# A cross network on one core: row halves that swap roles, one product split into seven smaller ones, and one-bank PSUM tiles

## The chip, the cores and the metric

The kernel runs on one core of a Trainium2 chip. Time is device time in microseconds (us) of one execution. The core has TensorE (matrix products, PE in the profile, its weight loads as PEld), VectorE (DVE), ScalarE (ACT), GpSimd (POOL) and SyncE (SP), each with its own queue of instructions worked off in order. All transfers of this kernel are issued from SyncE's queue.

## The reference

The input x0 has 16384 rows of 1024 elements in bf16. Six layers follow, each with a 1024x1024 weight matrix and a bias:

```python
x = x0
for l in range(6):
    proj = jnp.einsum('bd,de->be', x, ws[l]) + bs[l]
    x = x0 * proj + x
return x
```

So every layer is one product of 16384x1024 by 1024x1024, then an element-wise multiplication by x0 and an addition.

## The kernel before

The rows are worked in 16 pairs of two halves of 512 rows (`NPAIR`, `NB`). The data of a pair lie transposed in SBUF: 128 partitions of features, 8 blocks of features, 512 rows along the free dimension (`x0T`, and `xst` for the running x). A pair goes through all six layers before the next pair starts; a pair and layer together are called a step here, 96 of them.

In a step the 2x2 block product (two halves of the features by two halves of the rows, times two halves of the outputs) is done with seven half-size products instead of eight, in the manner of Strassen and Winograd. Each of the seven is 4 x 4 matmuls of 128x128 weights by 512 columns. With B(d, r) for feature half d and row half r, product 1 takes B(0,0), product 2 B(1,0), product 3 B(1,1), and products 5, 6, 7 and 4 take the differences T1 to T4, which VectorE makes (`emit_T`, lines 93 to 99): T1 = B(0,1) - B(0,0), T2 = B(1,1) - T1, T3 = B(1,1) - B(0,1), T4 = B(1,0) - T2. The weights of products 1, 2 and 4 are blocks of `ws`; those of 5, 6, 3 and 7 are combinations that VectorE makes once, in pair 0 (`emit_combo`, lines 126 to 132), for the layer that comes next, and saves to DRAM (`Lc`, line 106). All later pairs load seven weight tiles of 512 KB in each step through a ring of 12 buffers (`wring`, `prefetch_upto`, line 79), requested nine places ahead in the order of use.

The order in a step is 1, 5, 3, 2, 6, 7, 4. Matmuls are all on line 196. Product 1 starts two PSUM tiles of two banks each (`pA`); products 6, 7 and 4 add onto them one after the other, and after each of them ScalarE copies the running sum out (`evac`: line 205 without bias in pieces of 1024 columns, line 208 with bias in pieces of 512). Product 5 starts two other tiles (`pX`), product 3 adds onto them, and product 2 has the same pool's tiles after that. VectorE adds the evacuated parts (lines 235, 241, 250), multiplies by x0 (`final`, line 214) and adds the old x (line 223, in the last step line 219). In what follows "multiply" and "add" of a quarter (eh, n) are these two operations.

The queue of each engine is laid out in program order by the framework's scheduler, which may move instructions; semaphores are set by it. SyncE's queue holds the weight loads, the saves of combinations, per pair two transposing loads of x0 (lines 145 and 268), the output transpose (line 288) with two stores (line 291), and for the last pair four transposes (line 168) with four stores (line 280). A weight load waits until the product that used its ring slot has ended.

Of the kernel before, what the change touches and what calls it, by code (L numbers as in the profile page):

```python
# [16 lines left out]
def kernel(  # L17
# [19 lines left out]

    const = ctx.enter_context(tc.tile_pool(name="const", bufs=1))
# [7 lines left out]
    psA = ctx.enter_context(tc.tile_pool(name="psA", bufs=2, space=bass.MemoryType.PSUM))  # L46
    psX = ctx.enter_context(tc.tile_pool(name="psX", bufs=2, space=bass.MemoryType.PSUM))
    stage_ctx = ExitStack()
    w12_pool = stage_ctx.enter_context(tc.tile_pool(name="w12", bufs=2))
    xo_ctx = ExitStack()  # L50
    xo_pool = None

    Lc = dram.tile([L, 4, P, KH * H], BF16, name="Lc")
    CIDX = {5: 0, 6: 1, 7: 2, 3: 3}
# [11 lines left out]
    ORDER = [1, 5, 3, 2, 6, 7, 4]  # L66
    all_keys = [(pr, l, pid) for pr in range(NPAIR) for l in range(L) for pid in ORDER]
    key_pos = {k_: i for i, k_ in enumerate(all_keys)}
    is_dma = lambda k_: not (k_[0] == 0 and k_[2] in CIDX)
    PREF = 9  # L70
# [12 lines left out]
    def blk(t, dh, n):  # L83
        return t[:, n, dh * KH:(dh + 1) * KH, :]

    def emit_T(xsrc, which):
        B11, B12, B21, B22 = blk(xsrc, 0, 0), blk(xsrc, 0, 1), blk(xsrc, 1, 0), blk(xsrc, 1, 1)
        Ts = which["T"]
        for i in which["do"]:
            t_ = t_pool.tile([P, KH, NB], BF16, name=f"T{i}")  # L90
            Ts[i] = t_
            if i == 1:
                nc.vector.tensor_tensor(out=t_[:], in0=B12, in1=B11, op=SUB)  # L93
            elif i == 2:
                nc.vector.tensor_tensor(out=t_[:], in0=B22, in1=Ts[1][:], op=SUB)
            elif i == 3:
                nc.vector.tensor_tensor(out=t_[:], in0=B22, in1=B12, op=SUB)
            else:
                nc.vector.tensor_tensor(out=t_[:], in0=B21, in1=Ts[2][:], op=SUB)
# [4 lines left out]
    def flush_saves():  # L104
        for (l_, pid_, t_) in pending_saves:
            si = nc.sync.dma_start(Lc[l_, CIDX[pid_]].rearrange("p (k e) -> p k e", k=KH), t_[:])
            if state.get("last_dma") is not None:
                tc.add_manual_dep(si.ins, state["last_dma"].ins.name,
                                  mybir.DependencyInfo(mybir.DependencyClass.NoSync, mybir.DependencyReason.DATA),
                                  reason="combo save behind the urgent weight loads")  # L110
        pending_saves.clear()
# [8 lines left out]
    def emit_combo(l, pid):  # L120
        prefetch_upto(key_pos[(0, l, 4)] + 1)
        W11, W21, W22 = wtiles[(0, l, 1)], wtiles[(0, l, 2)], wtiles[(0, l, 4)]
        w12 = load_w12(l)
        t_ = wring.tile([P, KH, H], BF16, name="wp")
        if pid == 5:
            nc.vector.tensor_tensor(out=t_[:], in0=w12[:], in1=W22[:], op=ADD)  # L126
        elif pid == 6:
            nc.vector.tensor_tensor(out=t_[:], in0=wtiles[(0, l, 5)][:], in1=W11[:], op=SUB)  # L128
        elif pid == 3:
            nc.vector.tensor_tensor(out=t_[:], in0=W21[:], in1=wtiles[(0, l, 6)][:], op=SUB)  # L130
        else:
            nc.vector.tensor_tensor(out=t_[:], in0=W11[:], in1=w12[:], op=SUB)
        wtiles[(0, l, pid)] = t_
        pending_saves.append((l, pid, t_))

    wt0 = wring.tile([P, KH, H], BF16, name="wp")
    nc.sync.dma_start(wt0[:], w_src(0, 1))
    wtiles[(0, 0, 1)] = wt0
    load_w12(0)
    wt4 = wring.tile([P, KH, H], BF16, name="wp")  # L140
    nc.sync.dma_start(wt4[:], w_src(0, 4))
    wtiles[(0, 0, 4)] = wt4
    x0T_next = x0t_pool.tile([P, 2, KD, NB], BF16, name="x0T")
    for n in range(2):
        nc.sync.dma_start_transpose(out=x0T_next[:, n], in_=x0[n * NB:(n + 1) * NB, :])  # L145
    LK = L * KD
# [4 lines left out]
    for pid in (5, 6, 3, 7):  # L151
        emit_combo(0, pid)
    nc.gpsimd.tensor_copy(b_all[:], b_bf[:])
    Tn = {"T": {}, "do": (1, 2, 3, 4)}
    emit_T(x0T_next, Tn)
    prefetch_upto(PREF)
    flush_saves()

    for pr in range(NPAIR):
# [3 lines left out]
        xo_last = {"t": None, "regions": [], "xfin": None}  # L163

        def out_region(eh, n):
            if xo_last["t"] is None:
                xo_last["t"] = xo_pool.tile([P, 2, 2, KH, KH, P], BF16, name="xoS")
            ti = nc.sync.dma_start_transpose(out=xo_last["t"][:, eh, n].rearrange("p j k r -> p (j k) r"),
                                             in_=xo_last["xfin"][:, eh, n].rearrange("r j k p -> r (j k p)"))
            xo_last["regions"].append((eh, n))  # L170
            xo_last["tins"] = xo_last.get("tins", []) + [ti]
        for l in range(L):
            xsrc = x0T if l == 0 else xst
            Ts = Tn["T"]
            Tn = {"T": {}, "do": ()}
            rhs_of = {1: blk(xsrc, 0, 0), 2: blk(xsrc, 1, 0), 3: blk(xsrc, 1, 1), 4: Ts[4][:], 5: Ts[1][:], 6: Ts[2][:], 7: Ts[3][:]}
            bias_col = lambda eh, m: b_all[:, l * KD + eh * KH + m: l * KD + eh * KH + m + 1]
            if pr == 0 and l + 1 < L:
                prefetch_upto(key_pos[(0, l + 1, 4)] + 1)
                load_w12(l + 1)  # L180
            flush_saves()
            pA = [psA.tile([P, 2, NB], FP32, name="pa") for _ in range(2)]
            C1 = cb_pool.tile([P, KH, 2, NB], BF16, name="cb")
            C2 = cb_pool.tile([P, KH, 2, NB], BF16, name="cb")
            nxt_src = xst if l + 1 < L else None
            combos_next = pr == 0 and l + 1 < L

            def product(pid, pts, start):
                key = (pr, l, pid)
                prefetch_upto(key_pos[key] + PREF)  # L190
                wt = wtiles.pop(key) if not (pr == 0 and pid in (1, 2, 4)) else wtiles[key]
                rhs = rhs_of[pid]
                for m in range(KH):
                    for k in range(KH):
                        kw = {} if start else dict(skip_group_check=True)
                        nc.tensor.matmul(pts[m // 2][:, m % 2, :], lhsT=wt[:, k, m * P:(m + 1) * P], rhs=rhs[:, k, :],  # L196
                                         start=(start and k == 0), stop=(k == KH - 1), **kw)

            def evac(pts, bias_eh=None, dst=None):
                if dst is None:  # L200
                    e = ev_pool.tile([P, KH, NB], BF16, name="ev")
                    dst = e[:]
                if bias_eh is None:
                    for h in range(2):
                        nc.scalar.copy(out=dst[:, 2 * h:2 * h + 2, :], in_=pts[h][:])  # L205
                else:
                    for m in range(KH):
                        nc.scalar.activation(out=dst[:, m, :], in_=pts[m // 2][:, m % 2, :], func=IDENT,  # L208
                                             bias=bias_col(bias_eh, m), scale=1.0)
                return dst  # L210

            def final(Cb, eh, n):
                c = Cb[:, :, n, :]
                nc.vector.tensor_tensor(out=c, in0=c, in1=blk(x0T, eh, n), op=MULT)  # L214
                if last_pair and l == L - 1:
                    if xo_last["xfin"] is None:
                        xo_last["xfin"] = xst_pool.tile([P, 2, 2, KH, KH, P], BF16, name="xst")
                    v4 = lambda a: a.rearrange("r k (j p) -> r k j p", p=P)
                    nc.vector.tensor_tensor(out=xo_last["xfin"][:, eh, n].rearrange("r j k p -> r k j p"),  # L219
                                            in0=v4(c), in1=v4(blk(xsrc, eh, n)), op=ADD)  # L220
                    out_region(eh, n)
                else:
                    nc.vector.tensor_tensor(out=blk(xst, eh, n), in0=c, in1=blk(xsrc, eh, n), op=ADD)  # L223

            product(1, pA, True)
            P1s = evac(pA)
            pX = [psX.tile([P, 2, NB], FP32, name="px") for _ in range(2)]
            product(5, pX, True)
            P5s = evac(pX)
            product(3, pX, False)  # L230
            S53 = evac(pX, bias_eh=0)
            pX2 = [psX.tile([P, 2, NB], FP32, name="px") for _ in range(2)]
            product(2, pX2, True)
            P2s = evac(pX2, bias_eh=0)
            nc.vector.tensor_tensor(out=C1[:, :, 0, :], in0=P1s, in1=P2s, op=ADD)  # L235
            final(C1, 0, 0)
            if combos_next:
                emit_combo(l + 1, 5)
            product(6, pA, False)
            U2s = evac(pA)  # L240
            nc.vector.tensor_tensor(out=C1[:, :, 1, :], in0=U2s, in1=S53, op=ADD)  # L241
            final(C1, 0, 1)
            if nxt_src is not None:
                Tn["do"] = (1,)
                emit_T(nxt_src, Tn)
            if combos_next:
                emit_combo(l + 1, 6)
            product(7, pA, False)
            U3s = evac(pA, bias_eh=1)
            nc.vector.tensor_tensor(out=C2[:, :, 1, :], in0=U3s, in1=P5s, op=ADD)  # L250
            final(C2, 1, 1)
            if combos_next:
                emit_combo(l + 1, 3)
            product(4, pA, False)
            evac(pA, bias_eh=1, dst=C2[:, :, 0, :])
            final(C2, 1, 0)
            if nxt_src is not None:
                Tn["do"] = (2, 3, 4)
                emit_T(nxt_src, Tn)
# [63 lines left out]
```

## Time and profile before

| what | value |
|---|---|
| time, median of 3 runs | 2353.55 us (2353.24 to 2353.8) |
| span of the profiled execution | 2352.8 us, 0.75 us below the median |
| TensorE busy | 2312.4 us, 98% of the span |
| weight loads busy | 1052.7 us, 10752 loads, 98 ns each |
| VectorE busy | 1708.6 us, 73% |
| ScalarE busy | 1556.7 us, 66% |
| granted TensorE clock, mean | 0.997 of full speed |
| DMA | 457.96 MB, 67.0% of 16 engines' time |

A line of the costliest groups reads: line of the kernel, engine, operation, output tile <- input tiles, shapes, number of instructions, busy time in us, mean duration in ns, then the engine's idle time just before these instructions and what ended most of it. A line of waits reads: waiting engine, line, what it waited for, us in total, how often, the longest. In the timeline a row has start, duration, engine, line, operation, and in brackets the idle time before it. Matmuls overlap: a single record lasts 379 ns, while the next one starts long before its end, so the distance between starts tells the pace.

### The profile page before, as it was taken

To read this page: it belongs to the slowest core of one execution; us is meant where nothing else is said; L and a number is where in the kernel's file an instruction comes from. 1 tells how busy PE (TensorE), PEld (TensorE's weight loads), DVE (VectorE), ACT (ScalarE), POOL (GpSimd) and SP (SyncE) were. 2 spreads that over 40 slices of the span, in tenths; PEclk is the share of its full clock that TensorE was granted. 3 is DMA by queue.
4 is the path that set the end of the run, shared out by engine and by line. 5 is a ranking of instruction groups with operands and counts; after the bars stand their busy time and mean duration, and the time that the engine had idled before them with its cause. 6 is when DMAs were issued, how large, how long until landed. Compare 5 with 4: busy or idle time off the path is not lost.

```text
span 2352.8 us, 27562 instructions
## 1 busy us (share of the span) xinstructions
PE 2312.4 (98%) x10537; PEld 1052.7 (45%) x10752; DVE 1708.6 (73%) x1464; ACT 1556.7 (66%) x2113; POOL 1.2 (0%) x5
## 2 busy tenths in 40 slices
PE   7999999999999999999999999999999999999997
PEld 3444444444444444444444444444444444444443
DVE  5977767676777767676776767677776767777675
ACT  4666666666666666666666666666666666666665
POOL 0000000000000000000000000000000000000000
PEclk9999999999999999999999999999999999999998
DMA  7769485584956849568494774947749476594843
GB/s 226 203 210 256 152 216 196 161 253 154 228 184 171 241 154 240 171 177 235 153 259 153 178 233 152 259 152 190 221 152 260 153 198 214 155 257 152 226 153 86
DMA packets 599987, 457.96 MB, mean 195 GB/s; under 512 B 398128, under 2 KB 550704, under 8 KB 599856
## 3 DMA queue, kind: packets, MB, share of 16 engines
q1 hardware_dynamic: 599856, 456.20, 67.0%
q8 instruction: 85, 1.39, 0.2%
q14 instruction: 46, 0.38, 0.1%
HBM read 342.88 MB, written 46.14 MB: 165 GB/s over the span
## 4 chain that ended last, share of the span: by engine, by line
PE 96%; DVE 1%; DMA 1%; issue 1%; SPq 1%; ACT 0%; another core or an unknown queue 0%; DVEq 0%
PE pa L196 54%; PE px L196 42%; SPq L145 1%; DMA w_313<-in_ws_dram 0%; DMA wp<-in_ws_dram 0%; DVE cb L214 0%; DVE xst L219 0%; DVE xst L223 0%; ACT ev L208 0%; DVE cb L241 0%; DVE cb L250 0%; DVE cb L235 0%; DVE wp L128 0%; DVE T_247 L93 0%; DVE T_811 L93 0%
## 5 line engine op out<-in xcount | busy, mean ns | idle before, releaser
L196 PEld LDWEIGHTS <-wp 128*128 128x128 bf16 x10752 | 1052.7, 98 | 1283.8 <-issue 12.7
L208 ACT ACTIVATE ev<-px,b_all 128x512 bf16<-128x512 f32 x768 | 486.3, 684 | 201.3 <-PE px L196 193.3
L196 PE MATMUL px<-xst,wp 128*128 128x512 bf16 x2510 | 562.5, 379 | 2.7
L235 DVE TENSOR_TENSOR cb<-ev 128x2048 bf16<-128x2048 bf16 x96 | 117.6, 1225 | 594.2 <-ACT ev L208 594.2
L205 ACT CAST ev<-pa 128x1024 bf16<-128x1024 f32 x384 | 388.6, 1012 | 240.2 <-PE pa L196 230.8
L214 DVE TENSOR_TENSOR cb<-cb,x0T 128x2048 bf16<-128x2048 bf16 x384 | 467.8, 1221 | 6.3
L223 DVE TENSOR_TENSOR xst<-cb,xst 128x2048 bf16<-128x2048 bf16 x316 | 385.0, 1222 | 14.5
L208 ACT ACTIVATE ev<-pa,b_all 128x512 bf16<-128x512 f32 x384 | 243.1, 684 | 112.9 <-PE pa L196 108.2
L208 ACT ACTIVATE cb<-pa,b_all 128x512 bf16<-128x512 f32 x384 | 243.1, 684 | 88.4 <-ACT ev L208 48.4
L196 PE MATMUL pa<-xst,wp 128*128 128x512 bf16 x1254 | 287.3, 379 | 1.3
L205 ACT CAST ev<-px 128x1024 bf16<-128x1024 f32 x192 | 194.3, 1012 | 138.1 <-PE px L196 133.1
L241 DVE TENSOR_TENSOR cb<-ev 128x2048 bf16<-128x2048 bf16 x96 | 117.0, 1219 | 0.0
L250 DVE TENSOR_TENSOR cb<-ev 128x2048 bf16<-128x2048 bf16 x96 | 117.0, 1218 | 0.0
L196 PE MATMUL px<-x0T,wp 128*128 128x512 bf16 x501 | 112.4, 379 | 0.5
L223 DVE TENSOR_TENSOR xst<-cb,x0T 128x2048 bf16<-128x2048 bf16 x64 | 78.3, 1223 | 1.5
L196 PE MATMUL pa<-x0T,wp 128*128 128x512 bf16 x251 | 60.2, 391 | 12.9 <-DMA x0T<-in_x_dram 12.6
L130 DVE TENSOR_TENSOR wp<-wp 128x2048 bf16<-128x2048 bf16 x6 | 7.3, 1219 | 2.1 <-DMA wp<-in_ws_dram 2.1
L128 DVE TENSOR_TENSOR wp<-wp 128x2048 bf16<-128x2048 bf16 x6 | 7.3, 1219 | 0.0
L126 DVE TENSOR_TENSOR wp<-w_90,wp 128x2048 bf16<-128x2048 bf16 x1 | 1.2, 1226 | 8.2 <-DMA wp<-in_ws_dram 8.2
L93 DVE TENSOR_TENSOR T_111<-x0T 128x2048 bf16<-128x2048 bf16 x1 | 1.2, 1226 | 5.7 <-DMA x0T<-in_x_dram 5.7
L219 DVE TENSOR_TENSOR xst<-cb,xst 128x2048 bf16<-128x2048 bf16 x4 | 4.9, 1225 | 0.1
L196 PE MATMUL px<-T_247,wp 128*128 128x512 bf16 x16 | 3.6, 378 | 0.3 <-DVE T_247 L93 0.3
(783 smaller groups left out, 1858.9 us busy)
## 6 DMA issues: line engine op xcount, KB each, us to landing
wp<-Lc SPq DMA_DIRECT2D x360, 512.0 KB, 3.4
wp<-in_ws_dram SPq DMA_DIRECT2D x288, 512.0 KB, 3.7
out_dram<-x0T SPq DMA_DIRECT2D x30, 1024.0 KB, 9.8
Lc<-wp SPq DMA_DIRECT2D x24, 512.0 KB, 3.1
out_dram<-xoS SPq DMA_DIRECT2D x4, 512.0 KB, 4.7
w_90<-in_ws_dram SPq DMA_DIRECT2D x1, 512.0 KB, 4.7
x0T<-in_x_dram SPq DMA_TRANSPOSE x32, 7.3
w_130<-in_ws_dram SPq DMA_DIRECT2D x1, 512.0 KB, 5.0
```

The source lines that it names most:

```text
L128: nc.vector.tensor_tensor(out=t_[:], in0=wtiles[(0, l, 5)][:], in1=W11[:], op=SUB)
L130: nc.vector.tensor_tensor(out=t_[:], in0=W21[:], in1=wtiles[(0, l, 6)][:], op=SUB)
L145: nc.sync.dma_start_transpose(out=x0T_next[:, n], in_=x0[n * NB:(n + 1) * NB, :])
L196: nc.tensor.matmul(pts[m // 2][:, m % 2, :], lhsT=wt[:, k, m * P:(m + 1) * P], rhs=rhs[:, k, :], start=(start and k == 0), stop=(k == KH - ...
L205: nc.scalar.copy(out=dst[:, 2 * h:2 * h + 2, :], in_=pts[h][:])
L208: nc.scalar.activation(out=dst[:, m, :], in_=pts[m // 2][:, m % 2, :], func=IDENT, bias=bias_col(bias_eh, m), scale=1.0)
L214: nc.vector.tensor_tensor(out=c, in0=c, in1=blk(x0T, eh, n), op=MULT)
L219: nc.vector.tensor_tensor(out=xo_last["xfin"][:, eh, n].rearrange("r j k p -> r k j p"), in0=v4(c), in1=v4(blk(xsrc, eh, n)), op=ADD)
L223: nc.vector.tensor_tensor(out=blk(xst, eh, n), in0=c, in1=blk(xsrc, eh, n), op=ADD)
L235: nc.vector.tensor_tensor(out=C1[:, :, 0, :], in0=P1s, in1=P2s, op=ADD)
L241: nc.vector.tensor_tensor(out=C1[:, :, 1, :], in0=U2s, in1=S53, op=ADD)
L250: nc.vector.tensor_tensor(out=C2[:, :, 1, :], in0=U3s, in1=P5s, op=ADD)
```

## The change

Six things change.

1. The row half that has role 0 in one layer has role 1 in the next (`flip`), through a new class `Ops` that hands out the blocks and differences.
2. The order of the products becomes 1, 2, 5, 3, 6, 7, 4.
3. In pairs 1 to 15 product 2 is itself done as seven products of half its size: 256x256 weights by 256 columns, four matmuls of 256 columns each, 28 in place of 16 of 512 columns. Its input differences (`inner_t`, 128x512 elements each) and its weight combinations (number 8, made in pair 0 and loaded as an eighth tile per step) are new. Its seven results are copied into two tiles EA and EB and summed by VectorE. The small products lie among those of products 1 and 5, in three one-bank tiles: `q1` takes four groups, each adding onto the last after a copy, `q5` two, `q2` one.
4. PSUM is two pools of four one-bank tiles that change places from step to step. ScalarE's copies are all of 512 columns, and the bias of product 2's part goes to product 1's copies.
5. VectorE's sums for two of the quarters come in halves, and the order of VectorE's and ScalarE's instructions is pinned as written (`tc.keep_in_program_order`). The combinations 5, 6 and 3 of the next layer are made together after the first quarter.
6. At the start, the transposing load of the first half of x0 goes second in SyncE's queue; the weights of product 2, the second half, the block W12 and later the weights of product 4 follow. The look-ahead becomes 10.

```diff
--- before
+++ after
...
+    pin = tc.keep_in_program_order
+
+    def vtt(out, in0, in1, op):
+        return pin(nc.vector.tensor_tensor(out=out, in0=in0, in1=in1, op=op))
+
+    def acopy(out, in_):
+        return pin(nc.scalar.copy(out=out, in_=in_))
+
+    def abias(out, in_, bias):
+        return pin(nc.scalar.activation(out=out, in_=in_, func=IDENT, bias=bias, scale=1.0))
+
+    NQ = NB // 2
+    HE = H // 2
...
-    psA = ctx.enter_context(tc.tile_pool(name="psA", bufs=2, space=bass.MemoryType.PSUM))
-    psX = ctx.enter_context(tc.tile_pool(name="psX", bufs=2, space=bass.MemoryType.PSUM))
+    ti_pool = ctx.enter_context(tc.tile_pool(name="tip", bufs=1))
+    ei_pool = ctx.enter_context(tc.tile_pool(name="eip", bufs=1))
+    ps = [ctx.enter_context(tc.tile_pool(name=f"ps{i}", bufs=KH, space=bass.MemoryType.PSUM)) for i in range(2)]
...
-    ORDER = [1, 5, 3, 2, 6, 7, 4]
-    all_keys = [(pr, l, pid) for pr in range(NPAIR) for l in range(L) for pid in ORDER]
+    ORDER = [1, 2, 8, 5, 3, 6, 7, 4]
+    all_keys = [(pr, l, pid) for pr in range(NPAIR) for l in range(L) for pid in ORDER if pr > 0 or pid != 8]
...
-    PREF = 9
+    PREF = 10
...
+        elif pid == 8:
+            i11, i12 = W21[:, 0:2, 0:HE], W21[:, 0:2, HE:H]
+            i21, i22 = W21[:, 2:4, 0:HE], W21[:, 2:4, HE:H]
+            iv = t_[:].rearrange("p k (j e) -> p k j e", e=HE)
+            vtt(iv[:, 0], i12, i22, ADD)
+            vtt(iv[:, 3], i11, i12, SUB)
+            vtt(iv[:, 1], iv[:, 0], i11, SUB)
+            vtt(iv[:, 2], i21, iv[:, 1], SUB)
...
+    class Ops:
+        def __init__(self, x, flip, small):
+            b = lambda dh, r: x[:, r ^ flip, dh * KH:(dh + 1) * KH, :]
+            self.B = {(dh, r): b(dh, r) for dh in range(2) for r in range(2)}
+            self.T = {}
+            self.small = small
+            self.ti = None
+
+        def t(self, i):
+            B, T = self.B, self.T
+            T[i] = t_pool.tile([P, KH, NB], BF16, name=f"T{i}")
+            in0, in1 = {1: lambda: (B[0, 1], B[0, 0]), 2: lambda: (B[1, 1], T[1][:]),
+                        3: lambda: (B[1, 1], B[0, 1]), 4: lambda: (B[1, 0], T[2][:])}[i]()
+            vtt(T[i][:], in0, in1, SUB)
+
+        def inner_t(self, which):
+            if not self.small:
+                return
+            if self.ti is None:
+                self.ti = ti_pool.tile([P, 4, 2, NQ], BF16, name="ti")
+            ti, b = self.ti, self.B[1, 0]
+            b11, b12 = b[:, 0:2, 0:NQ], b[:, 0:2, NQ:NB]
+            b21, b22 = b[:, 2:4, 0:NQ], b[:, 2:4, NQ:NB]
+            for i in which:
+                in0, in1 = {1: (b12, b11), 2: (b22, ti[:, 0]), 3: (b22, b12), 4: (b21, ti[:, 1])}[i]
+                vtt(ti[:, i - 1], in0, in1, SUB)
...
+    x0T_next = x0t_pool.tile([P, 2, KD, NB], BF16, name="x0T")
+    LK = L * KD
+    nc.sync.dma_start_transpose(out=x0T_next[:, 0], in_=x0[0:NB, :])
+    wt2 = wring.tile([P, KH, H], BF16, name="wp")
+    nc.sync.dma_start(wt2[:], w_src(0, 2))
+    wtiles[(0, 0, 2)] = wt2
+    nc.sync.dma_start_transpose(out=x0T_next[:, 1], in_=x0[NB:2 * NB, :])
     load_w12(0)
-    wt4 = wring.tile([P, KH, H], BF16, name="wp")
-    nc.sync.dma_start(wt4[:], w_src(0, 4))
-    wtiles[(0, 0, 4)] = wt4
-    x0T_next = x0t_pool.tile([P, 2, KD, NB], BF16, name="x0T")
-    for n in range(2):
-        nc.sync.dma_start_transpose(out=x0T_next[:, n], in_=x0[n * NB:(n + 1) * NB, :])
-    LK = L * KD
     b_bf = const.tile([P, LK], BF16, name="b_bf")
     nc.sync.dma_start_transpose(out=b_bf[:], in_=bs.rearrange("l (m p) -> (l m) p", p=P))
     b_all = const.tile([P, LK], FP32, name="b_all")
     prefetch_upto(7)
...
+            flip = l % 2
+            small = pr > 0
...
+            psA, psX = ps[step % 2], ps[1 - step % 2]
+            step += 1
...
+            def inner(pt, w, rhs, start):
+                for m in range(2):
+                    for k in range(2):
+                        nc.tensor.matmul(pt[:, m * NQ:(m + 1) * NQ], lhsT=w[:, k, m * P:(m + 1) * P], rhs=rhs[:, k, :],
+                                         start=(start and m == 0 and k == 0), stop=(k == 1), skip_group_check=True)
...
+                q2, q5, q1 = bank(), bank(), bank()
+                for m in range(3):
+                    mm(1, w1, pA, m, True)
+                    ev(P1s, pA, m, 0)
+                inner(q1, w2[:, 0:2, 0:HE], b[:, 0:2, 0:NQ], True)
+                evi(EA[:, c11[0], c11[1]], q1)
+                inner(q5, wi[:, 0], ti[:, 0], True)
+                evi(EB[:, c22[0], c22[1]], q5)
+                mm(1, w1, pA, 3, True)
+                ev(P1s, pA, 3, 0)
+                inner(q2, w2[:, 2:4, 0:HE], b[:, 2:4, 0:NQ], True)
+                evi(EB[:, c11[0], c11[1]], q2)
+                pX = [bank() for _ in range(KH)]
+                w5 = weights(5)
+                mm(5, w5, pX, 0, True)
+                ev(P5s, pX, 0)
+                inner(q1, wi[:, 1], ti[:, 1], False)
+                evi(EA[:, c12[0], c12[1]], q1)
+                inner(q5, wi[:, 2], b[:, 2:4, NQ:NB], False)
+                evi(EB[:, c12[0], c12[1]], q5)
+                mm(5, w5, pX, 1, True)
+                ev(P5s, pX, 1)
+                inner(q1, wi[:, 3], ti[:, 2], False)
+                evi(EA[:, c22[0], c22[1]], q1)
+                mm(5, w5, pX, 2, True)
+                ev(P5s, pX, 2)
+                inner(q1, w2[:, 2:4, HE:H], ti[:, 3], False)
+                evi(EA[:, c21[0], c21[1]], q1)
+                w3 = weights(3)
+                mm(3, w3, pX, 0, False)
+                ev(S53, pX, 0, 0)
+                mm(5, w5, pX, 3, True)
+                ev(P5s, pX, 3)
+                for m in range(1, KH):
+                    mm(3, w3, pX, m, False)
+                    ev(S53, pX, m, 0)
+                half_sum(EA, EA, EB, 0)
+                cur.t(3)
+                vtt(EA[:, c22[0], c22[1]], EA[:, c22[0], c22[1]], EB[:, c22[0], c22[1]], ADD)
+                cur.t(4)
+                vtt(C1[:, :, 0, :], P1s[:], EA[:], ADD)
...
-            nc.vector.tensor_tensor(out=C1[:, :, 1, :], in0=U2s, in1=S53, op=ADD)
-            final(C1, 0, 1)
-            if nxt_src is not None:
-                Tn["do"] = (1,)
-                emit_T(nxt_src, Tn)
-            if combos_next:
-                emit_combo(l + 1, 6)
-            product(7, pA, False)
-            U3s = evac(pA, bias_eh=1)
-            nc.vector.tensor_tensor(out=C2[:, :, 1, :], in0=U3s, in1=P5s, op=ADD)
-            final(C2, 1, 1)
-            if combos_next:
-                emit_combo(l + 1, 3)
-            product(4, pA, False)
-            evac(pA, bias_eh=1, dst=C2[:, :, 0, :])
-            final(C2, 1, 0)
-            if nxt_src is not None:
-                Tn["do"] = (2, 3, 4)
-                emit_T(nxt_src, Tn)
+                for pid in (5, 6, 3):
+                    emit_combo(l + 1, pid)
...
+            half_sum(C1[:, :, 1, :], U2s, S53, 0)
+            half_sum(C1[:, :, 1, :], U2s, S53, 1)
+            f_mul(C1, 0, 1)
+            f_add(C1, 0, 1)
...
+            if more:
+                ops.inner_t((1,))
+                ops.t(1)
+                ops.inner_t((2, 3, 4))
+            f_mul(C2, 1, 0)
+            f_add(C2, 1, 0)
+            if more:
+                ops.t(2)
...
```

## The prediction

> **What bounds the kernel now.** I read the page's busy times and its chain first, then the waits, then one layer of the timeline, then the costliest groups.
>
> ```profile
> PE 2312.4 (98%) x10537; PEld 1052.7 (45%) x10752; DVE 1708.6 (73%) x1464; ACT 1556.7 (66%) x2113; POOL 1.2 (0%) x5
> PE 96%; DVE 1%; DMA 1%; issue 1%; SPq 1%; ACT 0%; another core or an unknown queue 0%; DVEq 0%
> L196 PEld LDWEIGHTS <-wp 128*128 128x128 bf16 x10752 | 1052.7, 98 | 1283.8 <-issue 12.7
> L205 ACT CAST ev<-pa 128x1024 bf16<-128x1024 f32 x384 | 388.6, 1012 | 240.2 <-PE pa L196 230.8
> L208 ACT ACTIVATE ev<-pa,b_all 128x512 bf16<-128x512 f32 x384 | 243.1, 684 | 112.9 <-PE pa L196 108.2
> L214 DVE TENSOR_TENSOR cb<-cb,x0T 128x2048 bf16<-128x2048 bf16 x384 | 467.8, 1221 | 6.3
> ```
>
> TensorE is 96% of the chain. "Busy" alone could hide gaps, so the waits decide: apart from the first load (12.6 us) TensorE waits 0.3 us twice, while ScalarE waits for TensorE everywhere.
>
> ```profile
> DVE cb L235 <- ACT ev L208: 594.2, 96, 7.9
> ACT ev L205 <- PE pa L196: 230.8, 368, 14.2
> PE pa L196 <- DMA x0T<-in_x_dram: 12.6, 1, 12.6
> PE px L196 <- DVE T_247 L93: 0.3, 1, 0.3
> ```
>
> One stretch of the timeline (start, duration, engine, what) shows the pace, and one of the weight loads beside it:
>
> ```profile
> 1021.07 3.62 PE L196 MATMUL pa<-T_7620,wp 128*128 128x512 bf16 x16
> 1024.52 3.62 PE L196 MATMUL pa<-T_7622,wp 128*128 128x512 bf16 x16
> 1024.72 1.01 ACT L205 CAST ev<-pa 128x1024 bf16<-128x1024 f32 x1 [0.71 <-PE pa L196]
> 1026.45 1.26 ACT L208 ACTIVATE ev<-pa,b_all 128x512 bf16<-128x512 f32 x2 [0.72 <-PE pa L196]
> 1034.17 2.35 DVE L214 TENSOR_TENSOR cb<-cb,x0T 128x2048 bf16<-128x2048 bf16 x2
> ...
> 2336.49 1.23 DVE L214 TENSOR_TENSOR cb<-cb,x0T 128x2048 bf16<-128x2048 bf16 x1
> 2337.75 1.23 DVE L219 TENSOR_TENSOR xst<-cb,xst 128x2048 bf16<-128x2048 bf16 x1
> ```
>
> ```profile
> 13.01 0.15 PEld L196 LDWEIGHTS <-wp 128*128 128x128 bf16 x1 [0.28 <-issue]
> 13.44 0.15 PEld L196 LDWEIGHTS <-wp 128*128 128x128 bf16 x1 [0.28 <-issue]
> ...
> 1021.07 1.39 PEld L196 LDWEIGHTS <-wp 128*128 128x128 bf16 x7
> ```
>
> The first matmuls run at half clock, 0.43 us apart.
>
>
> A product of 16 matmuls starts every 3.453 us: 0.2158 us per matmul. 10752 of these are 2320 of the span's 2352.8; the rest is the first load, a half-clock start and the tail. A layer is 7 x 3.453 = 24.17 us. Seven loads in 1.39 us have the same spacing (6 x 0.2158 + 0.098): each begins with a matmul and ends about 116 ns before the next one.
>
> **The change, part by part.**
>
> *Product 2 on seven small products (90 layers, pairs 1 to 15).* 16 matmuls of 512 columns (3.453 us) become 28 of 256. At half clock (11 intervals from 13.01 to 17.71) matmuls start 0.427 us apart; half of that is 0.2135, so 0.0023 of the 0.2158 doesn't scale with columns. 256 columns: 0.2135/2 + 0.0023 = 0.109 us. From below: half the row, 0.1079. From above: a load that nothing hides, 0.107 + 0.098 = 0.205. The load ends 98 ns after the matmul before it starts, so at 109 it still fits, by 11 ns; I take 0.109. 28 x 0.109 = 3.05: minus 0.40 a layer, 90 layers: **-36 us**, all on the path, since TensorE is it. The layer becomes 23.77.
>
> *The waits this adds.* Four of the seven share a bank (q1), each group after ScalarE's copy of the one before; TensorE is in order, so all later products queue behind such a wait, and so does every engine fed by them. No row has a 512-element cast. Bounds: 0.506 us (half the 1024 one) and 0.684 (with bias, same size); I take the middle, 0.595, as both rows are equally near. Two biased ones take 1.26, so the next starts 0.1 before the last ends; a copy can start 0.20 us after the next matmul begins (1024.52 to 1024.72). TensorE's ends from the layer's start, in the order written in the diff (P1, P5: a quarter product of four matmuls, 0.863; q: four small ones, 0.436): three of P1 2.59, q1 3.03, q5 3.46, P1 4.33, q2 4.76, P5 5.63, q1 6.06, q5 6.50, P5 7.36, q1 7.80, P5 8.66, fourth q1. ScalarE from there, a copy each 0.495: P5 5.83, q1 6.33, q5 6.82, P5 7.56, q1 8.06, which ends 8.655; with 0.06 to TensorE (a vector result at 43.28, the matmul that waited for it at 43.34) 8.715 against 8.66: 0.05 late, 90 x 0.05 = **+5**. At 0.506 nothing waits; at 0.684 the copies queue, the fourth q1 is 0.25 late and the last of P5, which takes the q1 bank, 0.08: +30. The other bank waits have 0.3 us or more in hand.
>
> [...]
>
> *ScalarE's total.* One-bank tiles turn each pair of casts into four, and seven copies are new: 16 biased x 0.584 + 15 x 0.495 = 16.8 us of 23.8; the order keeps it from starving TensorE except above. P1's bias replaces P2's.
>
> *VectorE in pairs 1 to 15.* 13 long operations instead of 15 (two sums are split in halves), 5 halves, 5 quarters. Long ones start 1.135 apart (2.35 for two), 1.26 where one reads the last one's result (2336.49 to 2337.75): 5 x 1.135 + 8 x 1.26 = 15.8. Halves: between 0.57 and 1.13, quarters 0.28 and 1.13; with the small fixed share that 1.221 against 1.135 leaves, 0.60 and 0.36. Sum 15.8 + 3.0 + 1.8 = 20.6, under 23.8: hidden, cost nothing, as long as TensorE is the slower. Without cover: all short ones at 1.13 make 27.1, and the layer follows VectorE.
>
> *Swapped halves and the order 1, 2, 5, 3.* With P4 starting at 0: P7's last copy 0.95, sum 1.7, multiply 2.9, add 4.1 (input of the small products), T1 and the small differences to 6.7, multiply 7.9, add 9.2 (input of product 3), T2 10.4. TensorE needs these at 6.0, 8.2, 12.5 and 16.9: nearly 2 us and more in hand. T3 and T4 follow the small copies and come by 14.4, needed at 20.3 and 23.8. Nothing is gained there either: before, TensorE had no wait to remove.
>
> *PSUM roles swapped.* Product 1 no longer waits for product 4's copies; that wait is not in the list, so 0.
>
> *Loads.* One 512 KB tile more in a layer: at 196 GB/s for a share of 0.67, 1.8 us of all engines, so about 0.75. A ring slot is now refilled about 28 us before use (12 tiles at 8 a layer) instead of 38. SyncE's queue is the danger: from a pair's start, the output transpose waits for the last add (5.3), issues 9.6 (as in the queue's rows below), two loads, the output stores (from 16.9), two loads, the x0 transposes once the stores have landed (12.8 after their issue: 29.7) for 10.9, then at 40.6 the loads of the third layer's products 1 and 2, landing at 44, needed at 47.6 and 49.7. In hand: some 4 us. Cost 0, bound from above 14 pairs x 4 = 56 if it comes 8 us later.
>
> ```profile
> 1038.83 9.63 SPq L288 DMA_TRANSPOSE x0T<-xst  x1
> 1050.35 5.83 SPq L291 DMA_DIRECT2D out_dram<-x0T  x2
> 1063.11 10.86 SPq L268 DMA_TRANSPOSE x0T<-in_x_dram  x2
> ```
>
> *Pair 0.* Its products stay large. VectorE has 17 long operations (10 of them dependent), 4 halves and, for the new combination, 4 quarters a layer: 7 x 1.135 + 10 x 1.26 + 2.4 + 1.6 = 24.5 against 24.17: 0.35 over five layers, +1.7. At the start the transpose of x0 goes ahead of two weight loads (issued 1.25 instead of 2.33): first matmul 1.1 earlier. But product 4's weight, which the first combination reads, goes from third to seventh in the queue and lands near 20, where VectorE ran that combination at 8.2. Its backlog (three combinations, T2, a fourth, T3, T4, the sum and finals, three more) puts the first layer's second half at 39.4, with P4 done at 38.5: +0.9. Sum **+1.5**, bounds -1 and +6.
>
> *Tail.* The last multiply waits 0.6 us behind VectorE's add today; the order after leaves it ready when ScalarE is: **-0.5**.
>
> Sum: -36 + 5 + 1.5 - 0.5 = -30 on 2352.8: span 2323, and with the 0.75 by which the median of the runs is above the span, **2324 us**.
>
> **The rivals.**
> 1. *The small weight loads aren't hidden* (slower). 98 ns in 109 leaves 11; what a load needs beyond its record isn't in the trace, for at 512 columns it had 116 ns to spare. Place: each of 2520 small matmuls. 30 us / 2520 = 12 ns more than 109 each cancels the gain; with half of each load exposed, 2520 x 0.049 = 123, the time is 2447. For: no row has such a pace. Against: loads start with the matmul before, not after it. Chance 0.10.
> 2. *The q1 bank holds TensorE* as in the upper bound or a little more: 25 to 35 us given back, 2344 to 2354. For: the chain is tight at every step. Chance 0.10.
> 3. *SyncE's queue comes late* after the x0 transposes: beyond the 4 us each further us costs 14; 2 us late gives 2352, 4 us 2380. For: more traffic behind slow transposes. Against: after them the queue issued eight loads in 4.4 us (1074.07 to 1078.43). Chance 0.05.
> 4. *VectorE becomes the bound*: short operations averaging over 0.8 us; at 27.1 us a layer it is 90 x 2.9 = 260 slower. Against: the rows' long ones are mostly proportional. Chance 0.03.
> That the split doesn't happen is out: the changed kernel's instruction list has the 28 matmuls of 256 columns in 90 layers.
>
> **How the numbers follow.** Forecast (2313 to 2340, from no bank wait and a start without loss to most of the upper cast bound) 0.72; the rivals 0.28. A difference under 0.2% (4.7 us) can't be told from none. Faster: 0.72 and 0.08 of rival 2: 0.80; same: 0.02 of 2, 0.02 of 3 and 0.01 of 1: 0.05; slower 0.15. The range 2313 to 2346 adds the near part of rival 2.
>
> **What would show it.** Right: small matmuls 0.109 apart, a layer of 23.8 in pairs 1 to 15, TensorE's waits on ScalarE near 5 us in all, none on weights. Wrong: a small spacing over 0.12; waits on the ea or eb copies of 20 us; loads of products 1 and 2 as releasers at each pair's third layer; VectorE near 95% busy.

## The result

The changed kernel takes 2329.68 us (median of 4 runs, 2329.11 to 2331.35) beside 2353.68 for the kernel before: a ratio of 0.990, 95% interval 0.9886 to 0.9914. That is 24 us less where 30 were forecast, inside the range. The profiled execution has a span of 2329.6 us, 23.2 below the 2352.8 of before.

The page after answers the lines shown of before: busy times, the chain, the new groups. A group's numbers are busy us and mean ns of one, then the idle time before.

```profile
span 2329.6 us, 31728 instructions
...
PE 2295.6 (99%) x11832; PEld 1158.5 (50%) x11832; DVE 1988.8 (85%) x2220; ACT 1824.4 (78%) x2959; POOL 0.4 (0%) x5
...
PE 96%; DVE 2%; SPq 1%; DMA 1%; issue 0%; ACT 0%; DVEq 0%
...
L247 PEld LDWEIGHTS <-wp 128*128 128x128 bf16 x2520 | 246.7, 98 | 133.2 <-DMA wp<-Lc 5.4
L247 PE MATMUL px<-ti,wp 128*128 128x256 bf16 x1440 | 216.7, 273 | 5.0 <-DMA wp<-Lc 5.0
...
L44 ACT CAST ev<-px 128x512 bf16<-128x512 f32 x792 | 463.3, 585 | 179.1 <-PE px L241 166.8
```

TensorE is still the chain; VectorE and ScalarE have come closer to it. A layer is read from the timeline, as the distance between first products, and the small pace from two groups of four in a row:

```profile
1005.84 2.75 PE L241 MATMUL px<-xst,wp 128*128 128x512 bf16 x12
...
1011.46 0.60 PE L247 MATMUL px<-ti,wp 128*128 128x256 bf16 x4
...
1011.90 0.60 PE L247 MATMUL px<-xst,wp 128*128 128x256 bf16 x4
...
1012.34 1.03 PE L241 MATMUL px<-T,wp 128*128 128x512 bf16 x4
...
1029.63 0.59 PE L241 MATMUL px<-x0T,wp 128*128 128x512 bf16 x2
```

1029.63 - 1005.84 is 23.79 us, against 24.17 before; four small matmuls take 0.44, and over the whole trace small ones start 0.109 apart. No wait on ScalarE appears in TensorE's list of waits (waited for, us in total, times, longest). What does appear is new:

```profile
PE px L241 <- DMA x0T<-in_x_dram: 10.5, 1, 10.5
...
PE px L247 <- DMA wp<-Lc: 5.0, 1, 5.0
...
PE px L241 <- DVE wp L41: 3.3, 1, 3.3
...
PE px L241 <- DVE xst L41: 0.4, 2, 0.3
```

Where the 23.2 us come from, by the times between the weight loads with which the pairs begin in the two traces (the second load of each, because the very first one runs some us ahead of the first matmul): the first matmul starts 2.1 earlier (10.53 for 12.63); pair 0 takes 154.69 for 148.56, +6.1; pair 1 takes 150.47 for 145.04, +5.4; each of the other 14 takes 2.25 less (142.79 for 145.04), -31.5; the tail is 1.2 shorter.

The +6.1 is one wait of product 5 in the very first layer. The rows show what it waited for: product 4's weights reach VectorE at 22.11, and the first combination ends at 23.33.

```profile
19.18 2.42 ACT L47 ACTIVATE ev<-px,b_all 128x512 bf16<-128x512 f32 x4 [5.42 <-POOL b_all L190]
...
22.11 1.22 DVE L41 TENSOR_TENSOR wp<-w,wp 128x2048 bf16<-128x2048 bf16 x1 [4.28 <-DMA wp<-in_ws_dram]
...
23.39 6.47 PE L241 MATMUL px<-T,wp 128*128 128x512 bf16 x16 [3.34 <-DVE wp L41]
```

The product then takes 6.47 instead of 3.62: the clock has halved (granted 0.50 from 23.40 to 29.20). In pair 1 the same happens behind a late eighth tile; SyncE's queue shows why it is late. The output transpose and the stores of pair 0 stand ahead of its load, which is issued at 189.02 and lands at 198.0.

```profile
171.03 10.41 SPq L421 DMA_TRANSPOSE x0T<-xst  x1
...
182.76 6.17 SPq L424 DMA_DIRECT2D out_dram<-x0T  x2
...
189.02 6.51 SPq L93 DMA_DIRECT2D wp<-Lc  x5
...
198.02 1.03 PE L247 MATMUL px<-ti,wp 128*128 128x256 bf16 x4 [4.95 <-DMA wp<-Lc]
```

The stretches behind the two waits, by their granted clock (the column after POOL's), and two undisturbed stretches for comparison, after and before:

```profile
23.40:29.20 5.80, 5.80 (x14) 2.10 (x15) 5.77 (x6) 1.77 (x4) 0.00 (x0) 0.50 0.91 353
...
198.00:203.00 5.00, 4.98 (x20) 2.95 (x21) 0.00 (x0) 1.72 (x4) 0.00 (x0) 0.50 1.02 403
...
600.00:742.00 142.00, 142.00 (x742) 72.39 (x741) 122.22 (x138) 113.74 (x186) 0.00 (x0) 1.00 0.76 221
```

```profile
600.00:742.00 142.00, 141.31 (x647) 64.35 (x659) 102.11 (x89) 95.34 (x130) 0.00 (x0) 1.00 0.69 197
```

So each wait costs more than its length: 3.3 + 2.9 us at the start, 5.0 + 2.7 in pair 1 (that layer takes 31.48 for 23.80). Before pair 2 the same tile's load is issued at 312.43, ahead of the output transpose (321.49), and nothing waits for it.

### The profile page after: what moved, and what is told of

It reads as the page before. It is cut to its first block, busy times and chain, and to the rows that moved or that the text cites. A ratio compares the mean times of both kernels' runs of the same rounds, so it can differ in the third digit from the quotient of the medians.

```text
span 2329.6 us, 31728 instructions
## 1 busy us (share of the span) xinstructions
PE 2295.6 (99%) x11832; PEld 1158.5 (50%) x11832; DVE 1988.8 (85%) x2220; ACT 1824.4 (78%) x2959; POOL 0.4 (0%) x5
## 4 chain that ended last, share of the span: by engine, by line
PE 96%; DVE 2%; SPq 1%; DMA 1%; issue 0%; ACT 0%; DVEq 0%
PE px L241 84%; PE px L247 12%; DVE cb L41 1%; DVE wp L41 1%; DVE xst L41 0%; DMA wp<-Lc 0%; SPq L180 0%; DVE T L41 0%; DMA wp<-in_ws_dram 0%; SPq L184 0%; SPq L187 0%; ACT cb L47 0%; SPq L116 0%; SPq L182 0%; SPq L176 0%
## 5 line engine op out<-in xcount | busy, mean ns | idle before, releaser
L241 PE MATMUL px<-T,wp 128*128 128x512 bf16 x6144 | 1405.0, 380 | 3.3 <-DVE wp L41 3.3
L47 ACT ACTIVATE ev<-px,b_all 128x512 bf16<-128x512 f32 x1152 | 791.3, 687 | 225.6 <-PE px L241 212.0
L44 ACT CAST ev<-px 128x512 bf16<-128x512 f32 x792 | 463.3, 585 | 179.1 <-PE px L241 166.8
L41 DVE TENSOR_TENSOR cb<-ev 128x1024 bf16<-128x1024 bf16 (+1 forms) x390 | 263.1, 696 | 232.1 <-ACT ev L44 232.1
L41 DVE TENSOR_TENSOR xst<-cb,xst 128x2048 bf16<-128x2048 bf16 x320 | 392.0, 1225 | 22.4 <-PE px L241 0.5
L47 ACT ACTIVATE cb<-px,b_all 128x512 bf16<-128x512 f32 x384 | 263.6, 687 | 67.9 <-PE px L241 54.8
L247 PE MATMUL px<-ti,wp 128*128 128x256 bf16 x1440 | 216.7, 273 | 5.0 <-DMA wp<-Lc 5.0
L44 ACT CAST ea<-px 128x512 bf16<-128x512 f32 x360 | 211.7, 588 | 0.0
L41 DVE TENSOR_TENSOR T<-xst,T 128x2048 bf16<-128x2048 bf16 x160 | 195.5, 1222 | 8.3
L41 DVE TENSOR_TENSOR T<-xst 128x2048 bf16<-128x2048 bf16 x160 | 194.9, 1218 | 0.0
L44 ACT CAST eb<-px 128x512 bf16<-128x512 f32 x270 | 160.2, 593 | 6.1 <-PE px L247 6.1
```

Of the source, the lines that this page charges most:

```text
L41: return pin(nc.vector.tensor_tensor(out=out, in0=in0, in1=in1, op=op))
L44: return pin(nc.scalar.copy(out=out, in_=in_))
L47: return pin(nc.scalar.activation(out=out, in_=in_, func=IDENT, bias=bias, scale=1.0))
L241: nc.tensor.matmul(pts[m][:], lhsT=wt[:, k, m * P:(m + 1) * P], rhs=rhs[:, k, :], start=(start and k == 0), stop=(k == KH - 1), **kw)
L247: nc.tensor.matmul(pt[:, m * NQ:(m + 1) * NQ], lhsT=w[:, k, m * P:(m + 1) * P], rhs=rhs[:, k, :], start=(start and m == 0 and k == 0), sto ...
```

## The experiments

All change the new kernel. "First" is the start of the first matmul; pairs are times between their second weight loads, pair 2 standing for all later ones but the last, which ends with its last load.

| kernel | first | pair 0 | pair 1 | pair 2 | span | median |
|---|---|---|---|---|---|---|
| before | 12.63 | 148.56 | 145.04 | 145.04 | 2352.8 | 2353.68 |
| changed | 10.53 | 154.69 | 150.47 | 142.79 | 2329.6 | 2329.68 |
| e1_whole | 8.2 | 155.15 | 145.04 | 145.04 | 2353.6 | 2355.36 |
| e5_banks | 8.1 | 155.87 | 150.52 | 142.79 | 2328.4 | 2329.75 |
| e4_noswap | 8.5 | 161.64 | 154.36 | 149.60 | 2433.7 | 2435.45 |
| e6_cols128 | 10.0 | 155.34 | 149.47 | 143.15 | 2333.7 | 2335.60 |
| e2_start | 8.2 | 153.82 | 149.77 | 142.79 | 2325.7 | 2327.89 |
| e3_defer | 8.5 | 154.05 | 142.79 | 142.79 | 2319.2 | 2321.86 |
| e7_mended | 8.8 | 153.20 | 142.79 | 142.79 | 2318.7 | 2320.38 |
| e8_pool | 8.3 | 164.88 | 144.67 | 142.79 | 2331.8 | 2334.22 |
| e9_bias | 9.2 | 152.12 | 142.79 | 142.79 | 2318.0 | 2319.33 |

The first matmul moves by 2 us between kernels that start alike: the first transposing load took 4.88 us to issue in e2_start and 7.23 in the changed kernel. Part of an earlier start is lost while product 5 waits for something later: e5_banks starts 2.4 us ahead of the changed kernel, and its pair 0 ends 1.2 ahead.

### Which part gains

**e1_whole: all but the small products.**

```diff
-    all_keys = [(pr, l, pid) for pr in range(NPAIR) for l in range(L) for pid in ORDER if pr > 0 or pid != 8]
+    all_keys = [(pr, l, pid) for pr in range(NPAIR) for l in range(L) for pid in ORDER if pid != 8]
...
-            small = pr > 0
+            small = False
...
-                ops = Ops(x0T_next, 0, True)
+                ops = Ops(x0T_next, 0, False)
```

> Everything of the change except the seven small products: product 2 is one whole product in every pair, and no eighth tile is loaded. Theory (the gain is the columns that TensorE no longer streams): a layer of pairs 1 to 15 goes from 23.80 back to 24.17 us, a pair from 142.79 to 145.04; the start keeps its wait, and the wait for the eighth tile in pair 1 (5.0 us and the half clock after it, 7.7 together) goes: span 2329.6 + 15 x 2.25 - 7.7 = 2355.6. Rival (swapped halves, order and one-bank tiles shorten the layer by themselves): a layer below 24.1 and a span below 2350.

Layers of 24.17, pairs of 145.04 and no wait in pair 1. (Combination 8 is still made and saved in pair 0, though nothing loads it.) The span is 2353.6 (the first matmul was 2.3 earlier than in the changed kernel); the ratio to the kernel before is 1.0005 (0.9996 to 1.0015). The rest of the change gains nothing by itself.

**e5_banks: PSUM pools that keep their roles.**

```diff
-            psA, psX = ps[step % 2], ps[1 - step % 2]
+            psA, psX = ps[0], ps[1]
```

> The changed kernel with the two PSUM pools keeping their roles from step to step. Theory (product 1 never waited for product 4's copies, so the exchange hides nothing): layers of 23.80 and 2329.6 within 1 us. Rival (the exchange is what lets product 1 start at once): a wait of 0.2 to 0.7 us for ScalarE in each layer, 18 to 65 us in all.

2329.75 against 2329.68, layers of 23.80: the exchange of the pools hides nothing here.

**e4_noswap: row halves keep their roles.**

```diff
-            flip = l % 2
+            flip = 0
...
-                ops = Ops(xst, 1 - flip, small)
+                ops = Ops(xst, 0, small)
...
-                ops.inner_t((1,))
                 ops.t(1)
-                ops.inner_t((2, 3, 4))
             f_mul(C2, 1, 0)
             f_add(C2, 1, 0)
             if more:
+                ops.inner_t((1, 2, 3, 4))
                 ops.t(2)
```

> The changed kernel without the exchange of the row halves; the small differences move behind the add that makes their input, and T1 before them. Theory (the exchange earns nothing itself but makes product 2's operand early enough to go second): the add of product 2's operand ends 7.6 us after product 4's start and TensorE wants it at 6.0, so it waits 1.6 us in each layer of pairs 1 to 15 but the first of a pair: 75 x 1.6 = 120, and some 0.7 us in five layers of pair 0: span near 2453; the clock stays whole, since the waits are short. Rival (the order of VectorE's work or another slack absorbs it): 2330.

A layer grows to 24.83 to 24.97, by 1.0 to 1.2 us and not 1.6, and the median is 2435, not 2453. The mechanism is the expected one; the size was some 0.5 us a layer too high. The waits, and one of them in the timeline, 0.15 behind the end of the add it needs. The first layer of a pair, which was to be spared, waits too, for the small differences, which this edit makes later:

```profile
PE px L247 <- DVE xst L41: 69.0, 72, 1.0
...
PE px L247 <- DVE ti L41: 13.1, 15, 0.9
```

```profile
1025.74 1.22 DVE L41 TENSOR_TENSOR xst<-cb,xst 128x2048 bf16<-128x2048 bf16 x1
...
1027.11 0.60 PE L247 MATMUL px<-xst,wp 128*128 128x256 bf16 x4 [0.97 <-DVE xst L41]
```

Exchanging the halves thus earns no time over the kernel before, but the split in this order without it loses 82 us to that kernel (one run). Through these waits of 1 us the clock stays whole: the four small matmuls behind the one shown take 0.60, as in the changed kernel, and the mean granted clock of both runs is 0.995.

### How near the weight loads are

**e6_cols128: each small matmul in two.**

```diff
-                    for k in range(2):
-                        nc.tensor.matmul(pt[:, m * NQ:(m + 1) * NQ], lhsT=w[:, k, m * P:(m + 1) * P], rhs=rhs[:, k, :],
-                                         start=(start and m == 0 and k == 0), stop=(k == 1), skip_group_check=True)
+                    for h in range(2):
+                        for k in range(2):
+                            c0 = m * NQ + h * P
+                            nc.tensor.matmul(pt[:, c0:c0 + P], lhsT=w[:, k, m * P:(m + 1) * P], rhs=rhs[:, k, h * P:(h + 1) * P],
+                                             start=(start and m == 0 and k == 0 and h == 0), stop=(k == 1), skip_group_check=True)
```

> The changed kernel with each small matmul cut into two of 128 columns: the same columns and results, twice the weight loads (56 instead of 28 in a layer). It asks how much room the load had at 256 columns. Theory (a load takes its 98 ns from the start of the matmul before it, and the next matmul follows at once): 0.10 us a matmul, a layer 56 x 0.10 - 3.05 = 2.5 us longer, 90 layers +229: 2559. First rival (loads follow one another faster than their record says): between 0.056 and 0.09 us, +0 to +180. Second rival (a load needs more than its record): over 0.11, +280 and more, and then 256 columns were at the edge.

All but the first rival fall: a layer is 23.86, only 0.06 longer, although it has 28 more weight loads.

```profile
1009.10 1.09 PEld L249 LDWEIGHTS <-wp 128*128 128x128 bf16 x16
...
1009.31 0.61 PE L249 MATMUL px<-xst,wp 128*128 128x128 bf16 x8
...
1009.76 0.61 PE L249 MATMUL px<-ti,wp 128*128 128x128 bf16 x8
...
1010.20 1.03 PE L241 MATMUL px<-xst,wp 128*128 128x512 bf16 x4
```

Eight matmuls of 128 columns take 0.44 to 0.45, 0.056 each, and so do their loads, though the record of one load lasts 98 ns: the records overlap.

### Where the rest of the gain went

**e3_defer: the eighth tile's load.** Pair 0's output goes into the queue behind the loads of pair 1's second layer, and pair 2's x0 two layers later.

```diff
             w6 = weights(6)
+            while pending_out:
+                pending_out.pop()()
...
-            if l == (2 if pr == 0 else 0) and not last_pair:
+            if l == (2 if pr <= 1 else 0) and not last_pair:
...
+        def store_pair(pr=pr, x0T=x0T, xst=xst):
             xo = x0T[:].rearrange("p n k (j r) -> p (n k j) r", r=P)
-        nc.sync.dma_start_transpose(out=xo, in_=xst[:].rearrange("r n k b -> r (n k b)"))
+            ti_ = nc.sync.dma_start_transpose(out=xo, in_=xst[:].rearrange("r n k b -> r (n k b)"))
+            if pr == 0:
+                nosync(ti_, state["last_dma"], "first output behind the next layer's weight loads")
...
+        if pr == 0:
+            pending_out.append(store_pair)
+        else:
+            store_pair()
```

> The changed kernel with pair 0's output transpose and stores put into SyncE's queue behind the weight loads of pair 1's second layer, and the x0 load for pair 2 two layers later. Theory (the one wait of pair 1 comes from the eighth tile's load standing behind that transpose and the stores): the wait of 5.0 us and 2.7 us of half clock go, all layers of pair 1 take 23.8, span 2329.6 - 7.7 = 2322. Rival (the queue or the memory has no room in pair 1 whatever the order): another tile comes late, span over 2327.

Pair 1 takes 142.79, as all others; median 2321.86, 7.8 less than the changed kernel. The wait was queue order, and neither the memory nor the load itself was short of room. The tiles of the second layer now go ahead of the transpose:

```profile
171.38 3.54 SPq L93 DMA_DIRECT2D wp<-Lc  x5
...
174.98 13.13 SPq L425 DMA_TRANSPOSE x0T<-xst  x1
```

**e2_start: the order of the first loads.**

```diff
     nc.sync.dma_start_transpose(out=x0T_next[:, 0], in_=x0[0:NB, :])
+    load_w12(0)
+    wt4 = wring.tile([P, KH, H], BF16, name="wp")
+    nc.sync.dma_start(wt4[:], w_src(0, 4))
+    wtiles[(0, 0, 4)] = wt4
     wt2 = wring.tile([P, KH, H], BF16, name="wp")
...
-    load_w12(0)
...
-    ops.t(1)
     for pid in (5, 6, 3):
         emit_combo(0, pid)
+    ops.t(1)
```

> The changed kernel with the block W12 and the weights of product 4 put ahead of product 2's weights and of the second transposing load at the start, and the first combinations before T1. Theory (product 5 waits 3.3 us for the first combination, which waits for product 4's weights, and the idle time costs half the clock for 2.9 us more): both go, span 2329.6 - 6.2 = 2323.4, first matmul still near 10.5. Rival (the start's transfers share what they have, so that another load comes late instead): a wait of some us for T1 or product 2's weights, span over 2327.

A miss, and a muddled test: 2327.89, 1.8 less and not 6.2. The half clock and the wait for a combination are gone (granted 1.00 from 12.00 to 47.00), but the scheduler, which was not bound to TensorE's written order, put part of product 6 ahead of product 5 in the first layer, so that TensorE waited 2.5 us for T2; and layers 2 to 6 grew from 24.17 to 24.6 to 25.1. VectorE is what they follow, busy 99.01 of 102 us (the third of the busy times):

```profile
40.00:142.00 102.00, 99.68 (x453) 44.62 (x460) 99.01 (x103) 74.25 (x116) 0.00 (x0) 1.00 0.68 213
```

**e7_mended: both, in the written order.** To e2 and e3 together come `pin` around both matmul calls, which holds them in the written order, and the first saves of combinations after the second layer's loads are asked for.

```diff
     prefetch_upto(PREF)
-    flush_saves()
```

> The deferred output of pair 0 and the start's other load order together, with TensorE's matmuls kept in the written order and the second layer's weight loads ahead of two of the saves. Theory (the waits of pairs 0 and 1 were all queue order; after that VectorE sets pair 0's layers at 24.6): first matmul 8.2 (as in three of the runs), pair 0 28.2 + 5 x 24.6 = 151.2, all others 142.79, 15.3 behind the last matmul's start: 2316. Rival (the start is bound by its transfers, whatever their order): pair 0 stays at 154 and the span at 2319 as with the deferred output alone.

2320.38: no clear difference from e3 alone. Pair 0 is 153.2, not 151.2, and not by layers of 24.6 (they are 24.17) but by one more wait in the first: product 5 wants the PSUM banks of product 2, whose copies queue behind product 1's, which now carry the bias.

```profile
18.24 0.99 POOL L193 CAST b_all<-b_bf 128x48 f32<-128x48 bf16 x1 [17.80 <-DMA b_bf<-in_bs_dram]
...
19.27 2.42 ACT L47 ACTIVATE ev<-px,b_all 128x512 bf16<-128x512 f32 x4 [7.21 <-POOL b_all L193]
...
22.21 5.30 PE L244 MATMUL px<-T,wp 128*128 128x512 bf16 x16 [4.19 <-ACT ev L44]
```

**e9_bias: the same, biases first.** The load of the biases moves up, between the first transpose of x0 and W12.

```diff
+    b_bf = const.tile([P, LK], BF16, name="b_bf")
+    nc.sync.dma_start_transpose(out=b_bf[:], in_=bs.rearrange("l (m p) -> (l m) p", p=P))
     load_w12(0)
...
-    b_bf = const.tile([P, LK], BF16, name="b_bf")
-    nc.sync.dma_start_transpose(out=b_bf[:], in_=bs.rearrange("l (m p) -> (l m) p", p=P))
```

> The mended kernel with the transposing load of the biases ahead of W12, the weights of products 4 and 2 and the second half of x0. Theory (product 1's copies now carry the bias, so ScalarE can't start before the biases have come, product 2's copies queue behind it, and product 5 waits 4.2 us for their PSUM banks, which also halves the clock): product 5 starts when T1 is there, near 20.4 instead of 22.2, at full clock, 1.8 and 1.9 us less: span 2315. Rival (VectorE's list of combinations sets pair 0 whatever TensorE's start): layers 2 to 6 grow to 24.6 and the span stays over 2317.

Both were right in part. The first layer falls from 32.34 to 29.60 at full clock (1.00 from 15.00 to 24.00), product 5 starting 0.06 after T1; but layers 4 to 6 then run at 24.6 to 24.7, VectorE's pace, and give 1.7 us back. 2319.33 (ratio 0.9851, 0.9834 to 0.9867) is the lowest of all, though not clearly apart from e3 and e7. It is 10 us below the changed kernel.

```profile
20.20 1.23 DVE L41 TENSOR_TENSOR T<-x0T 128x2048 bf16<-128x2048 bf16 x1 [2.40 <-DMA x0T<-in_x_dram]
...
21.49 3.63 PE L244 MATMUL px<-T,wp 128*128 128x512 bf16 x16 [1.38 <-DVE T L41]
```

**e8_pool: combination 8 on GpSimd.** As e7, but the four operations of combination 8 on the inner weights run on GpSimd.

```diff
-            vtt(iv[:, 0], i12, i22, ADD)
+            gtt = lambda o, x, y, op: pin(nc.gpsimd.tensor_tensor(out=o, in0=x, in1=y, op=op))
+            gtt(iv[:, 0], i12, i22, ADD)
...
```

> The same, with the four operations of combination 8 in each layer of pair 0 on GpSimd instead of VectorE. Theory (VectorE sets pair 0's layers): 1.55 us a layer leave it, layers of 24.17, five times 0.43 less: 2 us under the run before it. Rival (GpSimd slows VectorE beside it, or its result comes late): no gain, or a loss.

A loss of 14 us. GpSimd, with VectorE busy beside it nearly all the time (6.56 of the 6.70 us from 65.00 to 71.70), needed 1667 ns for what VectorE does in 418, and while it ran VectorE's multiplies and adds took 2.06 us instead of 1.23.

```profile
62.43 6.80 POOL L134 TENSOR_TENSOR wp<-wp 128x512 bf16<-128x512 bf16 x4 [18.74 <-PE px L245]
...
63.03 2.06 DVE L41 TENSOR_TENSOR xst<-cb,xst 128x2048 bf16<-128x2048 bf16 x1
...
65.01 3.20 DVE L41 TENSOR_TENSOR cb<-ev 128x1024 bf16<-128x1024 bf16 x2
...
68.25 2.06 DVE L41 TENSOR_TENSOR cb<-cb,x0T 128x2048 bf16<-128x2048 bf16 x1
```

## Why the prediction was right or wrong

**The split, -36: right.** 0.109 us a small matmul is what was measured, and e1 shows that the columns are the whole gain: 90 layers x 0.375 (24.17 to 23.795) = 33.75 us, against the -31 of split and bank wait together.

**The bank wait, +5: right in kind, too large.** The copies took 585 to 593 ns by their destination (595 assumed, bounds 506 and 684), and the layer is 0.03 above the sum of its matmuls, so at most 2 to 3 us. The trace has it where it was forecast: the third q1 copy ends at 1014.47, the fourth q1 group starts at 1014.52, and the four matmuls ahead of that group take 0.89 us from start to start instead of 0.86.

**ScalarE's total, 16.8 of 23.8: too low.** 113.74 busy in 142 us is 19.1 a layer, because most copies stand alone and don't overlap (in the layer from 1005.84, 21 of 31 start 0.17 to 0.28 us after the end of the one before); it still costs nothing.

**VectorE in pairs 1 to 15, 20.6 of 23.8: right.** 122.22 busy in 142 us is 20.5 a layer. Two halves take 1.28, so they start 0.60 apart, as assumed.

**Swapped halves and PSUM roles, 0: right** by e1 and e5, with what e4 adds: the exchange of halves is what makes the order 1, 2 possible.

**Pair 0 and the start, +1.5: too low; +4.0 was measured (6.1 less the 2.1 of the earlier start).** The step that failed is "lands near 20": product 4's weights came at 22. What it did to TensorE wasn't followed either: the sum carried the backlog to the layer's end and missed that product 5 itself stands still, 3.3 us, and that the clock halves behind it, 2.9. With the forecast's own first matmul (11.5) and the 9.5 us that two products took, TensorE would have wanted product 5 near 21.0 and had its weights at 21.2; the wait grew by the 2.1 us of the late weights and by the start, which came 1.0 earlier than forecast. VectorE's 24.5 a layer was right, but in the changed kernel it shows only in the last two layers of pair 0 (24.6); layers 2 to 4 take 24.17. In e2, e3 and e9, where TensorE loses less in the first layer, it shows earlier. That TensorE's lateness gives VectorE a lead which it then uses up would fit this, but isn't shown: in e7 all later layers take 24.17 after a first layer of 32.34, against 32.99 in the changed kernel. And "P1's bias replaces P2's", costed at nothing, was false at the start: ScalarE waited 5.4 us for the biases, and e7 shows this as the next wait in line.

**The loads, 0: right for 14 pairs, wrong for one.** "A ring slot is now refilled about 28 us before use" was worked out for pairs that follow each other alike. It held between pairs 1 and 2, where the second layer's eighth tile was asked for at 312.43 and wanted near 342. Between pairs 0 and 1 the second layer's tiles stand behind the output in the queue. As the code reads, slots are held there by weights that combination 8 still reads and by its results until they are saved; no run tested this part. Loads late by the queue's order are the mechanism of rival 3, at a place it didn't name, and this cost 7.7 us (e3): the larger half of what the forecast missed on the slow side, 2.5 at the start being the rest, against which the bank wait and the tail gave back about 3.5.

**The tail, -0.5:** measured -1.2.

**The rivals.** The weight load (rival 1) is not near: e6 halves the columns again and the pace follows, 0.056 us a matmul. Its "11 ns" of room read a record's length as the time between loads. The clock stayed at 1.00 over 142 us with 28 small matmuls a layer. What did lower it were single idle stretches: to 0.50 at the waits of 3.3 and 5.0 us, and to 0.62 over the 3.40 us behind one of 2.5 in e8_pool. Of the signs named for a right forecast, "none on weights" failed, by the 5.0 us of pair 1, and the waits on ScalarE are too short for the list.

## What to carry to other kernels

Cutting matmuls to 256 columns cost TensorE about 1 ns of 109 each here, so a recursion that streams fewer columns pays as long as its inputs arrive in order; that order, not the arithmetic, is what the rest of such a change must provide. A steady-state sum should be followed by a walk through the first layer and the first change from one regime to the next, one queue at a time: both losses here sat there. Where TensorE stood idle for 3.3 to 5.0 us, the wait cost more than its length (the work behind it took 1.7 to 2.9 us longer, in e7_mended and the changed kernel), and mending one wait shows the next (a combination, a bias, VectorE's list), so the gain of each is less than its length.

## What the runs showed of the hardware

Weight loads of 128x128, recorded at 98 ns each, followed one another every 56 ns in e6_cols128, where the matmuls have 128 columns.

In the changed kernel TensorE's clock fell to half during each of its two long waits inside the kernel, 3.3 and 5.0 us: it was 0.50 from 22.4 to 29.2 us and from 196.4 to 203.2, 6.8 us each time. In e7_mended the product behind a wait of 4.2 us took 5.30 us, and 3.63 behind one of 1.4 in e9_bias, where the clock was 1.00 throughout (15.00 to 24.00). A wait of 2.53 us was followed by a lower clock (e8_pool, 0.62 from 71.80 to 75.20), one of 2.45 was not (e2_start, 1.00 from 19.70 to 25.00). Whether the length of the wait alone decides it was not shown.

In e8_pool VectorE was slowed on element-wise work in bf16 while GpSimd did such work: its 128x2048 operation went from 1.23 to 2.06 us, two of its 128x1024 ones in a row from 1.29 to 3.20. What GpSimd loses by it wasn't measured, as it never ran alone.
